# Chunks 1 and 2 of an attention and feed-forward kernel: their second matrix product by Strassen's seven products, with weights laid out by halves and other sums of weights on GpSimd

## The chip, the cores and the metric

The kernel runs on one core of a Trainium2 chip. A core has TensorE (matrix products into PSUM), VectorE, ScalarE and GpSimd (elementwise work), SyncE (SP, whose queue issues the DMAs here) and 16 DMA engines. The metric is the device time of one execution in microseconds (us). Less is better. The profile's names for the engines are PE (TensorE), PEld (its weight loads), DVE (VectorE), ACT (ScalarE), POOL (GpSimd) and SP.

## The reference

Eight sequences of 576 tokens go through windowed attention with eight heads of 64, and then through a feed-forward network with a hidden size of 2048.

```python
scores = scale * np.matmul(q, k.transpose(0, 1, 3, 2))
mask_plain = (rel >= 0) & (rel < window)                                # window 32, heads 0-3
mask_dil = (rel >= 0) & (rel < window * dilation) & (rel % dilation == 0)  # dilation 4, heads 4-7
...
attn = np.exp(scores - np.max(scores, axis=-1, keepdims=True))
attn = attn / (np.sum(attn, axis=-1, keepdims=True) + 1e-09)
out = np.matmul(attn, v)
...
h = x @ w_in                       # x: 4608 x 512, w_in: 512 x 2048
g = 0.5 * h * (1.0 + erf(h * inv_sqrt2))
return (g @ w_out).astype(np.float32)   # w_out: 2048 x 512
```

w_in and w_out come as 64-bit numbers, which the kernel decodes on the chip into a high and a low half in 32-bit form.

## The kernel before

**Tiling.** The 4608 tokens are nine chunks of 512: eight are the first 512 tokens of a sequence, the ninth holds the rests. A product keeps float32 accuracy by three passes (high by high, low by high, high by low), each of them 128x512 matmuls in fp32r. The weights are 16 tiles `weights[f]`, one for each 128 hidden columns. Each holds both layers, 512 numbers each, for both halves.

**Stages on TensorE.** Chunk 0 comes first, in an order written out by hand (`ORDER`): TensorE works on it while the weights are loaded, decoded by ScalarE (`k`, `j`) and VectorE (`w`), and while the attention of chunks 0 and 1 is worked out. A word such as `w13:v` is the next step of decoding tile 13 on VectorE; `h` and `o` are the first and second product for one tile on TensorE, `g` the GELU and its split into halves, `s l e i n t a x` the steps of attention (capitals for chunk 1). Then chunk 1 and chunk 2 are multiplied plainly from the weight tiles in SBUF (`chunk`, lines 995 and 1012), with 12 matmuls for each hidden tile and layer. The other six chunks go in three pairs (`two_chunks`): each layer is one Strassen step over the pair, that is seven products of half size (P1 to P7) instead of eight, for 8 hidden tiles of double width, with 6 matmuls each (lines 1135 and 1243), so 336 matmuls for a layer and a pair.

**What Strassen needs.** Four of the seven products take sums of weights. `prepare` makes them during chunks 1 and 2: two adds on GpSimd (line 722), four subtractions on VectorE (line 732), the high half on ScalarE (line 744), the low half on VectorE (line 747), and a DMA to a scratch in DRAM (`sums`). The plain parts go to DRAM too (`both`, `one`). Later the pairs fetch them as slabs (`ring`). On the token side, VectorE forms sums of x (line 1067) and of the hidden values (`sum_c`, line 1169), and each product's operand is split into halves by `split`: high on ScalarE (line 969), low on VectorE (line 976). Hidden values of a pair are kept as `c`, after their GELU on ScalarE (line 1119).

**What sets the order.** Behind `ORDER` a planner (`Flow`) places jobs on each engine by due times and costs; each engine runs its queue in that order, and waits where a semaphore says so. TensorE's own order is fixed by the program; at given times of its clock `pe` puts in visits of attention: the scores of two heads' pairs (line 332), and the products with the values (line 468 for chunk 2, 482 for later ones). The softmax between them (`attend`) is minimum (lines 366, 372), exponentials on ScalarE (line 380), inverse, scaling and transposes on VectorE (lines 389 to 422) and a move on ScalarE (line 841). For chunk 2 `xout` puts the result into the operand `x` (lines 500 and 503). Chunk 0's last copies out of PSUM are `store`.

Of the kernel before, what the change touches and what calls it, by code (L numbers as in the profile page):

```python
# [19 lines left out]
P = 128  # L20
# [18 lines left out]
ORDER = ("q0:d s0:p l0:v d0:d k0:a q1:d *36 s1:p w0:v l0:v w0:v w0:v d1:d k0:a q2:d q3:d w0:v e0:a e0:a j0:a k1:a v1:d "  # L39
# [17 lines left out]


class Flow:


    LAG, LAG_PE, TABLE, PULL, LATE, NEXT = 0.25, 0.5, 1.3, 0.06, 0.06, {"DVE": 0.1, "ACT": 0.03}
# [4 lines left out]
    def add(self, engine, time, do=None, after=(), due=0.0, begin=0.0, take=(), give=(), table="", land=0.0, issue=0.5):  # L67
        j = dict(engine=engine, time=time, do=do, after=list(after), due=due, begin=begin, take=list(take), give=list(give),
                 table=table, land=land, issue=issue, ready=0.0, then=[])
        self.jobs.append(j)  # L70
        return j
# [15 lines left out]
    def run(self):  # L87
# [7 lines left out]
        while there:  # L95
            best = None
            for j in there:
                at, e = self.start(j)
                if at is None:
                    continue  # L100
                turn = j["table"] not in ("", self.table)
                key = (round(at + self.PULL * max(0.0, j["due"] - at) - self.LATE * max(0.0, at - j["due"] - 2.0) + self.TABLE * turn, 2), j["due"])
                if best is None or key < best[0]:
                    best = (key, j, at + self.TABLE * turn, e)
# [30 lines left out]
        assert n == len(self.jobs), (list(self.held), [(j["engine"], j["due"], j["take"]) for j in there if j["engine"] != "DMA" or j["due"] < 480])  # L135
# [13 lines left out]
def attn_ffn(ctx: ExitStack, tc: tile.TileContext, qk, qk_lp, qk_ld, v, v_ld, w, outT):  # L149
# [85 lines left out]
    def weight_tile(f):  # L235
        if weights[f] is None:
            weights[f] = wpool.tile([P, 2, 2 * DM], F32R, tag="w", name="weight")
        return weights[f]

    def w_split(f):  # L240
        for cols in halves(f):
# [10 lines left out]
            nc.vector.scalar_tensor_tensor(weight_tile(f)[:, 1, cols], mid, 2.0 ** -36, t.bitcast(F32), op0=ALU.mult, op1=ALU.mult)  # L252

    def w_high(f):
        for cols in halves(f):
            e = yield
            copy(e, weight_tile(f)[:, 0, cols], raws[f][:, cols, 1].bitcast(F32))

# [162 lines left out]

    def turn_pe(s):
# [60 lines left out]
    def xout(s, px):  # L485
        yield {"ACT": 0.6}
        s.x = xg.tile([P, 2, N], F32R, tag="xg", name="x")
        if s.wide:
            put = []
            for b in range(2):  # L490
                src = px[:, :, b * 64:(b + 1) * 64].rearrange("p r (g i) -> p r g i", g=4)
                dst = [s.x[:, t].rearrange("p (r b i g) -> p r b g i", r=4, b=2, g=4)[:, :, b] for t in range(2)]
                put.append((src, dst))
        elif s.c < 2:
            put = [(s.px, [s.x[:, 0], s.x[:, 1]])]
# [911 lines left out]
```

## Time and profile before

| what | before |
|---|---|
| device time, 3 runs | 815.03, 816.36, 816.39 us, median 816.36 |
| profiled execution | 814.89 us, span 813.1 us |
| TensorE busy | 801.6 us, 99% of the span |
| VectorE, ScalarE, GpSimd busy | 598.7, 520.8, 57.3 us |
| DMA | 187 MB, mean 230 GB/s |

The profiled execution is one run; its span lies between its first and last instruction, and the remaining 1.8 us are around it. A busy share is an average over stages; the chain that ended last is the work that the end hung on, followed back from the last instruction. Matmuls are pipelined, so the time of one is read from a long run of them in the chain and not from the mean duration of a record.

### The profile page before, as it was taken

Reading aid. Unit: us, or ns where it says so; the run is one execution under the profiler, and the core shown is the slowest. Engines: PE = TensorE matmul, PEld = TensorE weight load, DVE = VectorE, ACT = ScalarE, POOL = GpSimd, SP = SyncE. Lnnn points to the kernel's source line nnn. Section 1 sums busy time; section 2 is a strip of 40 time slices with the busy share of each in tenths; the row PEclk is TensorE's granted clock in tenths of the full one; section 3 lists DMA queues with packets and bytes.
Section 4 is the critical chain, followed back from the end, with each engine's and each line's share of the span. In section 5 each row is a group of like instructions: output and inputs, shape, how many; then the busy total and the mean of one; then the engine's idle time right before and its main releaser. Section 6 shows DMA issues by size and latency. Waiting matters only on the chain.

```text
span 813.1 us, 19125 instructions
## 1 busy us (share of the span) xinstructions
PE 801.6 (99%) x7854; PEld 658.5 (81%) x7854; DVE 598.7 (74%) x1007; ACT 520.8 (64%) x1292; POOL 57.3 (7%) x78
## 2 busy tenths in 40 slices
PE   7999999999999999999999999999999999999998
PEld 5788888888888888888888887888888888888886
DVE  7999965877764846786798778866996853489673
ACT  8898853668865846888654479766754532565441
POOL 6000011513303100000000000000000000000000
PEclk9999999999999999999999999999999999999999
DMA  9972044877874788676784659759764399555102
GB/s 370 419 300 106 0 154 167 291 266 270 308 263 153 274 272 349 248 273 225 255 337 148 215 185 412 260 176 348 247 217 155 97 374 350 214 188 186 41 1 104
DMA packets 68647, 187.35 MB, mean 230 GB/s; under 512 B 4560, under 2 KB 33744, under 8 KB 56400
## 3 DMA queue, kind: packets, MB, share of 16 engines
q1 hardware_dynamic: 68560, 186.14, 63.0%
q8 instruction: 61, 1.00, 0.5%
q14 instruction: 26, 0.21, 0.1%
HBM read 144.44 MB, written 38.80 MB: 225 GB/s over the span
## 4 chain that ended last, share of the span: by engine, by line
PE 97%; ACT 2%; DMA 1%; DVE 0%; issue 0%; SPq 0%; DVEq 0%
PE ps L1135 28%; PE ps L1243 28%; PE ps L995 11%; PE ps L1012 11%; PE ps L514 6%; PE ps L534 5%; PE ps L332 3%; PE ps L482 2%; ACT sm L380 1%; PE ps L447 1%; DMA raw_w<-w 1%; PE ps L460 1%; PE ps L468 0%; ACT raw_w L233 0%; PE ps L429 0%; PE ps L318 0%
## 5 line engine op out<-in xcount | busy, mean ns | idle before, releaser
L1135 PE MATMUL ps<-parts,ring 128*128 128x512 f32 x1008 | 232.9, 391 | 0.0
L1243 PE MATMUL ps<-parts,ring 128*128 128x512 f32 x1008 | 230.4, 390 | 0.0
L1243 PEld LDWEIGHTS ps<-parts,ring 128*128 128x128 f32 x1008 | 188.8, 188 | 39.6 <-DVE parts L976 0.4
L1135 PEld LDWEIGHTS ps<-parts,ring 128*128 128x128 f32 x1008 | 188.2, 188 | 40.4 <-DVE c L1111 0.3
L969 ACT CAST parts<-c 128x512 fp32r<-128x512 f32 x168 | 100.9, 620 | 67.0 <-DVE parts L976 36.2
L976 DVE TENSOR_TENSOR parts<-c,parts 128x512 fp32r<-128x512 f32 x168 | 113.4, 688 | 31.5 <-ACT parts L969 30.1
L995 PE MATMUL ps<-x,weight 128*128 128x512 f32 x384 | 89.8, 391 | 0.0
L1012 PE MATMUL ps<-parts,weight 128*128 128x512 f32 x384 | 89.8, 391 | 0.0
L995 PEld LDWEIGHTS ps<-x,weight 128*128 128x128 f32 x384 | 71.5, 188 | 15.2
L1012 PEld LDWEIGHTS ps<-parts,weight 128*128 128x128 f32 x384 | 71.5, 188 | 15.2
L380 ACT ACTIVATE sm<-sm,st 128x64 f32<-128x64 f32 (+1 forms) x224 | 75.6, 340 | 7.6 <-DVE st L372 7.4
L1119 ACT ACTIVATE c<-c 128x512 f32<-128x512 f32 x96 | 57.7, 628 | 33.0 <-DVE c L1111 32.8
L1111 DVE TENSOR_TENSOR c<-c,ps 128x512 f32<-128x512 f32 x72 | 49.5, 688 | 27.6 <-PE ps L1135 25.1
L170 DVE COPY c<-ps 128x512 f32<-128x512 f32 x50 | 34.6, 692 | 46.7 <-PE ps L1135 46.3
L168 ACT COPY c<-ps 128x512 f32<-128x512 f32 x52 | 30.5, 587 | 57.4 <-PE ps L1135 50.0
L1169 DVE TENSOR_TENSOR c<-c 128x512 f32<-128x512 f32 x96 | 63.7, 684 | 0.0
L722 POOL TENSOR_TENSOR units<-weight 128x512 f32<-128x512 f32 x32 | 43.7, 1390 | 207.4 <-DVE g L526 99.6
L514 PE MATMUL ps<-x,weight 128*128 128x512 f32 x192 | 46.9, 394 | 0.0
L534 PE MATMUL ps<-g,weight 128*128 128x512 f32 x192 | 45.6, 390 | 0.0
L841 ACT COPY turned<-half 32x256 f32<-32x256 f32 x104 | 42.0, 404 | 5.5 <-DVE turned L422 4.0
L380 ACT ACTIVATION_READ_ACCUMULATOR sm<-sm,st 128x1 f32 x224 | 42.3, 189 | 0.0
L534 PEld LDWEIGHTS ps<-g,weight 128*128 128x128 f32 x192 | 36.0, 188 | 7.4
(99 smaller groups left out, 816.0 us busy)
## 6 DMA issues: line engine op xcount, KB each, us to landing
ring<-sums SPq DMA_DIRECT2D x48, 1024.0 KB, 6.5
ring<-both SPq DMA_DIRECT2D x24, 1024.0 KB, 6.9
v_sb<-v SPq DMA_DIRECT2D x17, 1024.0 KB, 9.2
raw_qk<-qk SPq DMA_DIRECT2D x32, 512.0 KB, 5.6
raw_w<-w SPq DMA_DIRECT2D x16, 1024.0 KB, 15.6
sums<-units SPq DMA_DIRECT2D x16, 1024.0 KB, 5.6
ring<-one SPq DMA_DIRECT2D x12, 1024.0 KB, 7.9
both<-weight SPq DMA_DIRECT2D x16, 512.0 KB, 6.6
```

The source lines that it names most:

```text
L380: nc.scalar.activation(t, s.sc[:, i // NU, at:at + 2 * KB] if s.c < 2 else t, AF.Exp, bias=s.st[:, 0, i:i + 1], scale=SCALE if s.c < 2 els ...
L514: nc.tensor.matmul(bank, weights[f][:, t, cc * P:(cc + 1) * P], x[:, xx], start=n == 0, stop=n == 3 * NC - 1)
L534: nc.tensor.matmul(ps[:, d], weights[f][:, t, DM + d * P:DM + (d + 1) * P], gs[f][:, u], start=first and n == 0, stop=last and n == 2)
L969: nc.scalar.copy(to if len(x.shape) == 2 else to.rearrange("p (g i) -> p g i", i=32), x)
L976: nc.vector.tensor_sub(a, x, b)
L995: nc.tensor.matmul(bank, weights[f][:, i, cc * P:(cc + 1) * P], x[:, j], start=n == 0, stop=n == 3 * NC - 1)
L1012: nc.tensor.matmul(ps[:, bank_of(acc[d])], weights[f][:, i, DM + d * P:DM + (d + 1) * P], made["g", c, f][:, j], start=f == 0 and n == 0, ...
L1111: nc.vector.tensor_add(C[f][:, part], C[f][:, part], ps[:, bank_of(bank)])
L1119: nc.scalar.activation(C[f][:, part], C[f][:, part], AF.Gelu)
L1135: nc.tensor.matmul(ps[:, bank_of(bank)], w()[:, a, i * P:(i + 1) * P], made[n, u, i][:, b], start=begins and k == 0, stop=k == 5, skip_gro ...
L1169: op(C[f][:, to], C[f][:, a], C[f][:, b])
L1243: nc.tensor.matmul(ps[:, bank_of((n, b, d))], w()[:, i, d * P:(d + 1) * P], made[key][:, j], start=begins and f == 0 and k == 0, stop=f == ...
```

## The change

Chunks 1 and 2 become a pair, pair 0, and there are four pairs. In pair 0 the first layer stays plain (a new branch for `n == 0` in `two_chunks`, line 1091 of the new file): 32 blocks of 12 matmuls, each with a GELU straight out of PSUM into `c` (line 1097). Its second layer takes the seven products as the other pairs do (line 1279). Chunk 2's attention comes earlier: scores and softmax of its first two pairs of heads stand at the end of `ORDER` (words with @), and the others in pair 0's first blocks.

A weight tile is now laid out by quarters with the high and low half side by side. Each tile is written to DRAM as it is decoded (`w_away`, words with z), 32 DMAs of 512 KB, which replace the 32 of `both` and `one`. Tiles 0 to 7 leave SBUF this way, and pair 0 fetches them back as `ring`. `prepare` now adds the high and low half of a tile on GpSimd (lines 778 and 784), and three VectorE subtractions follow in place of four (line 796). GpSimd's first add waits for the decoding of the last tile (`gate`). The high half may be made by VectorE too. The new names of the lines: 332, 380, 468, 841, 969, 976 and 1169 are now 370, 418, 516, 470, 1015, 1022 and 1198.

```diff
-    LAG, LAG_PE, TABLE, PULL, LATE, NEXT = 0.25, 0.5, 1.3, 0.06, 0.06, {"DVE": 0.1, "ACT": 0.03}
+    LAG, LAG_PE, TABLE, PULL, LATE, NEXT = 0.25, 0.5, 1.23, 0.02, 0.056, {"DVE": 0.1, "ACT": 0.03}
...
-            weights[f] = wpool.tile([P, 2, 2 * DM], F32R, tag="w", name="weight")
+            weights[f] = wpool.tile([P, 4, 2, DM // 2], F32R, tag="w", name="weight")
...
+    def w_away(t):
...
+        for layer in range(2):
+            to = drams["plain", layer, f // 4][2 * side:2 * side + 2, :, f % 4].rearrange("u p k -> p u k")
+            nc.sync.dma_start(to, weights[t][:, 2 * layer:2 * layer + 2].rearrange("p u t k -> p u (t k)").bitcast(F32))
...
-    NPAIRS = 3
+    NPAIRS = 4
...
+            turns = ((P1, every), (P4, every), (P2, range(4)), (P5, every), (P6, every), (P7, every), (P2, range(4, HALF)), (P3, every))
...
+        def join_side(side):
...
+            w = layer_0[f][side]() if layer == 0 else weights[tiles_of(f)[side]][:, 2:4]
+            nc.gpsimd.tensor_add(y(2 * side, 2 * side + 2), w[:, :, 0].bitcast(F32), w[:, :, 1].bitcast(F32))
...
+        if n == 0:
+            blocks = [(0, f) for f in range(5)] + [(1, f) for f in range(5)] + [(b, f) for f in range(5, HALF) for b in range(2)]
+            for b, f in blocks:
+                got = [fetch_layer_0(f)] if f > 3 else []
+                if b and f == 0:
+                    got += x_there["two", 0] + x_there["two", 2]
+                for side in range(2):
...
+                                nc.tensor.matmul(bank, column(w, i, cc), x[:, j], start=k == 0, stop=k == 3 * NC - 1)
...
+                        nc.scalar.activation(C[f][:, part], ps[:, bank_of(key)], AF.Gelu)
...
-    CH, PAIR = 384 * MM, 672 * MM
+    FIRST, PAIR = 720 * MM, 672 * MM
...
+    gate = const.tile([1, 8], F32)
+    nc.gpsimd.tensor_copy(gate, weights[NF - 1][0:1, 3, 1, 0:8].bitcast(F32))
+    for f in range(4):
+        prepare(1, f, 1.0 + 10.6 * f)
+        prepare(0, f, -1.2 + 8.0 * f)
+    for f in range(4, HALF):
+        prepare(1, f, 65.3 + 10.4 * (f - 4))
+        prepare(0, f, 76.6 + 11.4 * (f - 4))
-    chunk(1, ((0, 8), (8, 16)))
-    chunk(2, ((0, 8), (8, 16)))
```

TensorE's queue from the end of chunk 0 on, before (514, 534: chunk 0; 332: scores):

```order
L534 MATMUL ps<-g,weight 128x512 x36
L995 MATMUL ps<-x,weight 128x512 x12
L332 MATMUL ps<-raw_qk 32x64 x64
L995 MATMUL ps<-x,weight 128x512 x48
L332 MATMUL ps<-raw_qk 32x64 x64
L995 MATMUL ps<-x,weight 128x512 x36
L1012 MATMUL ps<-parts,weight 128x512 x12
```

The same place now (551 and 571 are chunk 0, 370 scores, 516 the products with the values):

```order
L571 MATMUL ps<-g,weight 128x512 x12
L370 MATMUL ps<-raw_qk 32x64 x64
L571 MATMUL ps<-g,weight 128x512 x24
L1091 MATMUL ps<-x,weight 128x512 x12
L370 MATMUL ps<-raw_qk 32x64 x64
L1091 MATMUL ps<-x,weight 128x512 x36
L516 MATMUL ps<-turned,v_sb 64x32 x64
L1091 MATMUL ps<-x,weight 128x512 x48
L1091 MATMUL ps<-x,ring 128x512 x12
L516 MATMUL ps<-turned,v_sb 64x32 x64
L1091 MATMUL ps<-x,ring 128x512 x12
L1091 MATMUL ps<-x,weight 128x512 x24
```

Chunk 2's first scores moved into chunk 0, and both of its products with the values now stand within the first nine blocks of pair 0.

ScalarE's queue between the second exponentials of chunk 2 and that second product, now (units are sums of weights, 1097 the GELU, 470 the move of the turned scores, 540 `xout`):

```order
L418 ACTIVATE sm_1798,st_1799<-sm_1798,st_1799 128x64 x3
L170 CAST units_1819<-units_1819 128x4x256
L1097 ACT_TABLE_LOAD
L1097 ACTIVATE c_1815<-ps_72 128x512
L1097 ACTIVATE c_1963<-ps_72 128x512
L170 CAST units_1917<-units_1917 128x4x256
L1097 ACTIVATE c_1963<-ps_72 128x512
L470 COPY turned_1986<-half_1970 32x256 x4
L1097 ACTIVATE c_2013<-ps_72 128x512
L470 COPY turned_2015<-half_1996 32x256 x4
L1097 ACTIVATE c_2013<-ps_72 128x512
L1097 ACTIVATE c_2095<-ps_72 128x512
```

Behind chunk 0 the same queue had before, with GELU and high half in turn:

```order
L1000 ACTIVATE gf_1619<-ps_72 128x512
L969 CAST parts_1624<-gf_1619 128x512
L1000 ACTIVATE gf_1644<-ps_72 128x512
L969 CAST parts_1647<-gf_1644 128x512
L1000 ACTIVATE gf_1667<-ps_72 128x512
L969 CAST parts_1671<-gf_1667 128x512
```

Two moves that TensorE's product waits for now stand behind casts for the sums of weights and GELUs.

VectorE's queue ahead of those two moves, now (796, 805: sums of weights; 443 to 460: scaling and transposes of the softmax):

```order
L443 TENSOR_TENSOR sm_1766<-sm_1766,st_1767 128x512
L805 TENSOR_TENSOR units_1819<-units_1819 128x4x256
L796 TENSOR_TENSOR units_1917<-units_1917 128x256
L427 TENSOR_SCALAR st_1799<-st_1799 128x8
L457 STREAM_TRANSPOSE half_1970<-sm_1766 128x256
L429 RECIPROCAL st_1799<-st_1799 128x8
L460 STREAM_TRANSPOSE turned_1986<-sm_1766 128x512
L443 TENSOR_TENSOR sm_1798<-sm_1798,st_1799 128x512
L805 TENSOR_TENSOR units_1917<-units_1917 128x4x256
L457 STREAM_TRANSPOSE half_1996<-sm_1798 128x256
L460 STREAM_TRANSPOSE turned_2015<-sm_1798 128x512
```

The low halves of two sums of weights stand between the steps of the softmax that the product waits for.

## Rows read from the trace of the kernel before

**Rows 1.** The page: busy time by engine, and TensorE's granted clock.
```profile
PE 801.6 (99%) x7854; PEld 658.5 (81%) x7854; DVE 598.7 (74%) x1007; ACT 520.8 (64%) x1292; POOL 57.3 (7%) x78
...
PEclk9999999999999999999999999999999999999999
```

**Rows 2.** Chain that ended last: start us, us, what.
```profile
118.11 8.16 PE ps L534 x36
126.27 2.72 PE ps L995 x12
128.99 1.41 PE ps L332 x91
...
188.30 2.00 PE ps L468 x128
...
411.34 46.24 PE ps L1243 x204
...
733.24 76.17 PE ps L1243 x336
```

**Rows 3.** Waits of TensorE, 126 to 814 us: total, times, longest.
```profile
PE ps L482 <- issue: 0.2, 1, 0.2
PE ps L332 <- issue: 0.2, 1, 0.2
```

**Rows 4.** Busy time by stretch, count in brackets; then clock, DMA share, GB/s.
```profile
24.00:126.30 102.30, 102.30 (x891) 84.79 (x886) 90.21 (x136) 82.62 (x157) 2.77 (x2) 1.00 0.46 182
126.30:324.90 198.60, 198.44 (x2561) 162.90 (x2560) 135.61 (x237) 134.21 (x384) 40.96 (x30) 1.00 0.76 266
...
411.30:491.10 79.80, 79.80 (x594) 65.61 (x593) 65.74 (x111) 44.72 (x102) 0.00 (x0) 1.00 0.61 218
```

**Rows 5.** ScalarE and VectorE by form: shape, count, busy us, mean ns, idle before.
```profile
L976 DVE TENSOR_TENSOR parts<-c,parts 128x512 fp32r<-128x512 f32 x168 | 113.4, 688 | 31.5 <-ACT parts L969 30.1
...
L1000 ACT ACTIVATE gf<-ps 128x512 f32<-128x512 f32 x32 | 19.1, 597 | 29.6 <-PE ps L995 28.1 <-DVE parts L976 1.5
...
L744 ACT CAST units<-units 128x1024 fp32r<-128x1024 f32 x16 | 16.7, 1044 | 1.7 <-issue 1.6
...
L380 ACT ACT_TABLE_LOAD x8 | 10.3, 1283 | 0.1
```

**Rows 6.** ScalarE in time: start us, us, instruction, idle before it.
```profile
154.86 0.35 ACT L380 ACTIVATE sm<-sm,st 128x64 f32<-128x64 f32 x1
155.11 0.19 ACT L380 ACTIVATION_READ_ACCUMULATOR sm<-sm,st 128x1 f32 x1
155.21 0.33 ACT L380 ACTIVATE sm<-sm,st 128x64 f32<-128x64 f32 x1
```

**Rows 7.** ScalarE in time, behind the product with the values.
```profile
190.36 1.08 ACT L500 CAST x<-ps 128x512 fp32r<-128x512 f32 x2 [0.78 <-PE ps L468]
191.47 1.65 ACT L841 COPY turned<-half 32x256 f32<-32x256 f32 x4
```

**Rows 8.** GpSimd's adds in time.
```profile
143.05 3.00 POOL L722 TENSOR_TENSOR units<-weight 128x512 f32<-128x512 f32 x2 [9.96 <-ACT parts L969]
...
184.81 3.52 POOL L722 TENSOR_TENSOR units<-weight 128x512 f32<-128x512 f32 x2 [5.22 <-DMA sums<-units]
```

**Rows 9.** VectorE in time, beside those adds.
```profile
143.56 1.34 DVE L976 TENSOR_TENSOR parts<-gf,parts 128x512 fp32r<-128x512 f32 x1
...
146.73 1.22 DVE L747 TENSOR_TENSOR units<-units 128x1024 fp32r<-128x1024 f32 x1
```

**Rows 10.** VectorE in time, beside the later adds.
```profile
185.15 2.04 DVE L747 TENSOR_TENSOR units<-units 128x1024 fp32r<-128x1024 f32 x1
187.11 1.78 DVE L976 TENSOR_TENSOR parts<-gf,parts 128x512 fp32r<-128x512 f32 x1
```

**Rows 11.** The page: DMA issues, KB each, median us to landing.
```profile
sums<-units SPq DMA_DIRECT2D x16, 1024.0 KB, 5.6
...
both<-weight SPq DMA_DIRECT2D x16, 512.0 KB, 6.6
```

More of the change, by code (lines that the diff above doesn't have):

```diff
@@ L134, in run @@
                     there.append(k)
-        assert n == len(self.jobs), (list(self.held), [(j["engine"], j["due"], j["take"]) for j in there if j["engine"] != "DMA" or j["due"] < 480])
+        assert n == len(self.jobs)
 def at_once(gen):
@@ L422, in turn, with moved, move @@
         nc.vector.transpose(s.t, x[:, :, 0].unsqueeze(1).broadcast_to((P, 2, 2 * NU, KB)))
+    def moved(s):
+        yield
+        move(s)
+    def move(s):
+        for r in range(4):
+            to = r ^ 1
+            nc.scalar.copy(s.t[32 * to:32 * to + 32, r % 2], s.half[32 * r:32 * r + 32])
     def turn_pe(s):
@@ L556, in job @@
         kind, i = name[0], name[1:]
+        if kind == "@":
+            p = int(i[1:])
+            if i[0] == "v":
+                return load_v(xs[2][p])
+            if i[0] == "S":
+                return together([scores(xs[2][p + k], 6) for k in range(2)])
+            return dict(l=lowest, e=softmax, i=inverse, n=norm, t=turn, m=moved)[i[0]](xs[2][p])
         if kind == "d":
@@ new lines, in attn_ffn, with fetch_layer_0, go @@
+    SUMS = ((P5, P4, P7, P6), (P5, P7, P4, P6))
+    IN_SUMS = SUMS[0]
+    PLAIN = ({P1: 0, P2: 1, P3: 3}, {P1: 0, P2: 2, P3: 3})
+    def slab_of(layer, u, i):
+        if u in IN_SUMS:
+            return drams["sums", layer, i][SUMS[layer].index(u)]
+        return drams["plain", layer, i][PLAIN[layer][u]]
+    put_in, joined, layer_0, fetched_0 = {}, {}, {}, {}
+    for f in range(4):
+        layer_0[f] = [lambda t=t: weights[t][:, 0:2] for t in tiles_of(f)]
+    def fetch_layer_0(f):
+        if f not in fetched_0:
+            st = {}
+            def go():
+                st["w"] = wpool.tile([P, 4, 2, NW1], F32R, tag="w", name="ring")
+                nc.sync.dma_start(st["w"].rearrange("p u t k -> p u (t k)").bitcast(F32),
+                                  drams["plain", 0, 1][:, :, f % 4].rearrange("u p k -> p u k"))
+            layer_0[f] = [lambda side=side: st["w"][:, 2 * side:2 * side + 2] for side in range(2)]
+            at = 22 + 6 * (f - 4) if f < 5 else 44 + 11 * (f - 4)
+            key = ("layer 0", f)
+            fetched_0[f] = flow.add("DMA", 2.6, go, [joined[k, f - 4] for k in range(2)], due=at - 8, begin=at - 20, take=[("w", key), ("ring", ("r",) + key)], land=2.3)
+        return fetched_0[f]
@@ L725, in plain @@
-        def plain():
-            one, two = (g, f) if layer == 0 else (f, g)
-            part = slice(cols.start + NW1, cols.stop) if layer == 0 else slice(cols.start, cols.start + NW1)
-            nc.sync.dma_start(drams["both", layer, half][:, f % 4 * 2:f % 4 * 2 + 2], weights[two][:, :, cols].bitcast(F32))
-            nc.sync.dma_start(drams["one", layer, half][:, f % 4 * 2:f % 4 * 2 + 2], weights[one][:, :, part].bitcast(F32))
-        def both(op, to, a, b):
-            return lambda: op(y(to), y(a), y(b))
@@ L733, in prepare @@
-        sums = []
-        for i in range(2):
-            sums.append(flow.add("POOL", 1.35, add_up(i), sums[:], due - 6, due - 12,
-                                 [] if i else [("prep", key + ("prep",)), ("w", key)]))
-        away = [flow.add("DMA", 2.0, plain, due=due, begin=due - 12, land=2.3, issue=1.2)]
-        sub, add = nc.vector.tensor_sub, nc.vector.tensor_add
-        j = sums
-        for op, to, a, b in ((sub, B22, B22, B12), (sub, B12, B12, B11), (add, B11, B22, B11), (sub, B21, B21, B11)):
-            j = [flow.add("DVE", 0.37, both(op, to, a, b), j, due - 3)]
@@ L894, in attend @@
             up = ("upper", c, p, 0)
-            visit = flow.add("PE", 1.45, pe_work([scores(s, 6), scores(t, 6)]), q, take=[("upper", up)], give=[x for _, x in keys])
-            visits.append((scores_at[0], visit))
+            visit = q is not None and flow.add("PE", 1.45, pe_work([scores(s, 6), scores(t, 6)]), q, take=[("upper", up)], give=[x for _, x in keys])
+            if visit:
+                visits.append((scores_at[0], visit))
             lows = []
-            for i, o in enumerate(pairs):
+            for i, o in enumerate(pairs if visit else ()):
                 low, tt = softmax_of(i, o, [visit], scores_at[0] + i * 1.4, exps_at[i])
@@ L1401 @@
     out = r.results[0]["outT"].T
-    one, two = out[:3 * N].reshape(3, N, DM), out[3 * N:].reshape(3, 2, 2, 8, 32, DM)
-    two = two.transpose(0, 2, 3, 1, 4, 5).reshape(6, N, DM)
-    chunks = np.concatenate([one, two], 0)
+    chunks = out.reshape(NCH, N, DM)
     parts = chunks[:B], chunks[B].reshape(B, REST, DM)
```

357 lines of the change are left out of this document (177 added, 180 removed), and 36 rows, old and new, of the table ORDER.

## The prediction

> **What bounds the kernel now.** I read the page first. TensorE is busy for 99% of the span and its granted clock is at the top in each slice [rows 1]. Busy records overlap, so that share proves little, and I went on to the chain that ended last. From 118 us to the end it is made of TensorE's runs alone, one behind the other: chunk 0's last products, the plain products of chunks 1 and 2, the visits of attention, and the Strassen layers [rows 2]. The waits of TensorE say the same from the other side: between 126 and 814 us it waited for no other engine, and its two entries of 0.2 us are its own issue [rows 3]. So each matmul that goes away is worth its whole time, as long as nothing else becomes late. A run of 336 matmuls takes 76.17 us in the last layer [rows 2], which is 0.2267 us for one.
>
> The second thing to read is how much room the engines have that feed TensorE. In the stretch of chunks 1 and 2 VectorE is busy for 135.6 of 198.6 us, with 237 instructions (0.572 us each), and in the second Strassen layer of the pair behind it for 65.7 of 79.8 us, with 111 instructions (0.592 us each) [rows 4]. There TensorE waited for nothing at 82%.
>
> **The change part by part.**
>
> *What is removed.* Before, chunks 1 and 2 took 768 large matmuls, 384 for each layer. Now the first layer keeps 384 and the second takes 7 products of 8 tiles with 6 matmuls, 336. In all, TensorE's queue holds 3120 large matmuls in place of 3168; the small ones of attention are the same in number. 48 x 0.2267 = 10.9 us off the path. That follows from the order and is not in doubt. Against the profiled execution (814.9 us) this gives 804.0, and against the median of the three runs (816.4, which is 1.5 us above the profiled one) 805.5. I go by the median.
>
> *What is moved into chunk 0.* The scores of chunk 2's first pairs cost 1.41 us wherever they stand [rows 2]. Their exponentials now come ahead of pair 0. Chunk 0's h15 ends at 118.1 us [rows 2]; o13, the scores, o14 and o15 follow, 3 x 2.72 + 1.41, and a few tenths behind the scores, so pair 0 begins at F = 127.8 us. On ScalarE 16 exponentials take 0.33 us each, since each one's reading of the sum overlaps the next [rows 6], so 5.3 us, behind a table load of 1.28 us [rows 5] that can run early. With two moves of 1.65 us [rows 7], the VectorE steps between them and two copies out of PSUM, I get ScalarE free at about F + 6.0. The GELUs that wait behind this free PSUM banks. Six banks hold six blocks of 2.72 us, 16 us, so TensorE doesn't notice. I cost this at nothing; without those banks it would be 6.0 - 2.7 = 3.3 us.
>
> *Chunk 2's second product with the values.* This is where a wait is likeliest. It stands behind 108 large matmuls, one scores visit of 1.41 us and one product of 2.00 us, so at F + 28.3 with the few tenths behind each visit. On ScalarE there stand, between F + 6.0 and the move that it needs: four casts for sums of weights (1.04 us each), three table loads (1.28 each), seven GELUs (0.60 each) [rows 5], 16 exponentials (5.3), two casts of x (1.08) and two moves (3.3) [rows 6, 7]. Together 4.2 + 3.8 + 4.2 + 5.3 + 1.1 + 3.3 = 21.9, so F + 27.9. The margin is 0.4 us. VectorE has 34 instructions between the scores (F + 4.3) and the last transpose; at 0.572 us each 19.4 us of the 22 us to F + 26.3, where the last move has to start. Both queues are nearly full, and they hand work to each other.
>
> Here GpSimd matters. Beside its adds VectorE is slower: a subtraction that takes 0.69 us [rows 5] took 1.34 within two adds [rows 8, 9], 0.33 us for an add, and beside two later adds a low half took 2.04 in place of 1.22 and a subtraction 1.78 in place of 0.69 [rows 5, 8 to 10], 0.95 us for an add. By the order GpSimd has 12 adds that can run before F, and four whose buffers only come free from the first puts (5.6 us to land [rows 11]), which puts them into this stretch. Four adds at 0.33 to 0.95 us cost 1.3 to 3.8 us, less the margin 0.9 to 3.4; if they fall into gaps, nothing. I take 0.6 us for an add, between the rows, so 2.4 - 0.4 = **2.0 us**. The operand x of chunk 2 comes out of this product: ScalarE and VectorE need some 2.5 us, and one block of 2.72 us stands in front of the block that reads it. I cost it at nothing; it is late by what exceeds 0.2 us.
>
> *The rest of pair 0's first layer.* It lasts 87.1 us of matmuls and ten visits (5 x 1.41 + 2 x 2.00 + 3 x 1.41), 102.3 us. VectorE's 129 instructions make 73.8 us by 0.572. The later products with the values have 2 us of room and more by the same way of counting, and a wait of 2 us earlier adds to that. Nothing.
>
> *The second layer of pair 0.* 76.2 us of matmuls and three visits give 80.4 us. VectorE's queue from the first split of the hidden values to the last has 129 instructions, at 0.592 us each 76.4 us, or 95%. Some of that can run before the layer begins, since chunk 1's hidden values are ready early. I take nothing, with 0 to 3 us for the range.
>
> *The DMAs.* The 32 writes of plain weights, 512 KB each [rows 11], go from the stretch of chunks 1 and 2 into chunk 0, where the DMA engines were busy for 46% [rows 4]. In SP's queue two loads of weights and the loads of chunk 2 now stand behind some of them. The tiles written first had been decoded long before, so SP doesn't wait for them; if it did, the decoding of tiles 12 and 14 would wait with it. The 22 more slab loads of 1 MB go into a stretch at 76%, less what moved out. Nothing.
>
> Sum: 816.4 - 10.9 + 2.0 = **807.5 us**.
>
> **The rivals.**
>
> *A: no new wait.* The adds fall into gaps of VectorE: 805.5 us. For it speaks that the planner's queues left TensorE without a wait in every stage of before [rows 3]; against it that no stage of before had ScalarE without a gap for 22 us ahead of a product.
>
> *B: VectorE becomes the bound in the second layer.* If its instructions take 0.65 us there (0.688 us is the mean of a split alone [rows 5], neighbours overlap), 129 make 83.9 us for 80.4 us; with the same late start as in the forecast that is 4 to 7 us, so 812 us. Against it: at 82% there was no wait at all.
>
> *C: the sums of weights come late.* The second layer's products P4 need slabs of sums, 10.9 us into the layer. A slab has GpSimd, VectorE, ScalarE, a put of 5.6 us and a fetch behind it, and all stand in queues with the softmax. If the last tiles were late by some 10 us the gain would be gone: 816 us, no change. By the order the last put stands two visits ahead of the layer, which speaks against it.
>
> *D: GpSimd holds VectorE for the whole of each add, and more adds fall here.* The first 12 adds wait for buffers that chunk 0's last products free. If they too slip behind F, and each add of 1.5 us [rows 8] holds VectorE for its whole length, 12 adds cost 18.0 - 0.4 = 17.6 us: 823 us, slower. It is slower than before by over 0.2% (818.0) from 9 adds on (9 x 1.5 - 0.4 = 13.1 us lost against 10.9 gained). Against it speak the rows: 0.65 us lost beside two adds, 1.9 beside two others, not 3.0.
> [...]
>
> **How the numbers follow.** Forecast 0.55, A 0.18, B 0.13, C 0.07, D 0.07. The range takes the forecast's bounds (805.5 + 0 to 3.4, and 0 to 3 in the second layer), A and most of B: 804.8 to 813.5, where the lower end is A less 0.7 us, half the spread of the three runs. A measurement of this kernel can tell about 0.2% (1.6 us) from no change. Faster by more: the forecast, A and B, 0.86; within it: C, 0.07; slower: D, 0.07.
>
> **What would show it.** Right: in the chain of waits TensorE waits once for ScalarE's move, about 28 us into pair 0, for 1 to 3 us, and else for nothing over 1 us; the run of pair 0's second layer has 336 matmuls in 76 us apart from its visits; VectorE is over 90% busy there. Wrong: TensorE waiting for VectorE's splits all through the second layer (B), for a slab behind a put (C), or VectorE's two-input instructions beside GpSimd at twice to three times their length in the first 28 us (D). If the clock fell in some stretch for a wait, the matmuls would take longer than 0.2267 us there, and the sum would be wrong in its first term.

## The result, and the profile after

| kernel | device time, median (us) | runs | ratio to before, 95% interval |
|---|---|---|---|
| before | 815.8 (814.8 to 817.1) | 11 | |
| changed | 820.7 (816.2 to 823.4) | 11 | 1.0056 (1.0043 to 1.0070) |

The change made the kernel slower by 0.56%; the forecast was 1.1% faster. Its runs spread over 7.2 us, those of before over 2.3, and the mean granted clock of its runs lies between 0.987 and 0.996. What follows is the account of one of them, the profiled one (0.992). Its execution took 819.8 us, with a span of 817.9 us against 813.1. The page now shows 48 large matmuls fewer, as worked out, TensorE no longer covering the span, and VectorE at 652.8 us in place of 598.7 [rows 1].

```profile
span 817.9 us, 19149 instructions
...
PE 799.4 (98%) x7806; PEld 655.3 (80%) x7806; DVE 652.8 (80%) x1072; ACT 531.7 (65%) x1305; POOL 60.5 (7%) x75
...
q8 instruction: 61, 1.00, 0.5%
```

The waits of TensorE between 126 and 814 us, which were 0.4 us before [rows 3], come to 7.6 us (columns: instruction, what it waited for, total us, times, longest):

```profile
PE ps L508 <- issue: 4.0, 2, 2.2
PE ps L1279 <- ACT sm L418: 2.2, 1, 2.2
PE ps L530 <- ACT parts L1015: 0.7, 1, 0.7
PE ps L516 <- ACT turned L470: 0.5, 1, 0.5
PE ps L370 <- issue: 0.2, 1, 0.2
```

The stage lengths say where the time went. From the first matmul of a stage to the first of the next, in us, with the pairs numbered as in the changed kernel:

| stage | before | changed | what was expected |
|---|---|---|---|
| pair 0 (chunks 1 and 2), both layers | 198.6 | 195.1 | 188.2 |
| pair 1, both layers | 166.2 | 165.5 | 166.2 |
| pair 2, first layer | 85.3 | 85.3 | 85.3 |
| pair 2, second layer | 80.7 | 88.2 | 80.7 |
| pair 3, both layers | 152.1 | 152.1 | 152.1 |

The expected 188.2 is 198.6 less 10.9, less 1.5 for the scores that moved into chunk 0 (1.41 and a tenth behind them), plus the 2.0 of the forecast wait. Two places lost what was missing: 6.9 us in pair 0, and 7.5 us in a stage that the change doesn't touch; pair 1 gave 0.7 back.

**The untouched stage.** In pair 2's second layer stand the two visits of chunk 8's products with the values, 192 small matmuls each (line 508, before 460). Here is TensorE in time around them, first in the kernel before (start us, us, instruction, number of matmuls):

```profile
580.40 2.11 PE L460 MATMUL ps<-turned,v_wide 32*64 32x32 f32 x192
582.44 9.81 PE L1243 MATMUL ps<-parts,ring 128*128 128x512 f32 x42
592.19 2.04 PE L460 MATMUL ps<-turned,v_wide 32*64 32x32 f32 x186
```

and then in the changed kernel, where in brackets stands the idle time ahead of a row:

```profile
577.51 1.77 PE L508 MATMUL ps<-turned,v_wide 32*64 32x32 f32 x156
581.04 0.57 PE L508 MATMUL ps<-turned,v_wide 32*64 32x32 f32 x36 [1.76 <-issue]
581.54 14.19 PE L1279 MATMUL ps<-parts,ring 128*128 128x512 f32 x54
595.66 1.83 PE L508 MATMUL ps<-turned,v_wide 32*64 32x32 f32 x165
599.69 0.66 PE L508 MATMUL ps<-turned,v_wide 32*64 32x32 f32 x27 [2.20 <-issue]
```

Both visits stop in the middle, behind 156 and 165 matmuls, and wait for nothing that the profile can name ("issue"). From 578.3 us until TensorE went on at 581.04 the DMA engines moved nothing but one packet of the queue that the page calls "instruction", and that one had landed at 579.56. This is the DMA view of 578.3 to 579.4 us:

```profile
DMA packets 1, 0.02 MB, mean 15 GB/s; under 512 B 0, under 2 KB 0, under 8 KB 0
...
q8 instruction: 1, 0.02, 5.5%
```

And behind each stop the granted clock fell from 1.00 to 0.50 for 3.41 us (582.69 to 586.10 and 599.76 to 603.17). In the changed kernel by stretch (us; busy time of TensorE, its weight loads, VectorE, ScalarE and GpSimd with counts; granted clock; DMA share; GB/s):

```profile
578.90:580.70 1.80, 0.38 (x37) 0.26 (x24) 1.80 (x4) 0.00 (x0) 0.00 (x0) 1.00 0.00 0
...
582.50:585.90 3.40, 3.40 (x11) 2.57 (x10) 1.38 (x2) 1.20 (x4) 0.00 (x0) 0.53 0.91 316
```

The second row is the stretch at half clock. It lies in a run of 54 large matmuls, which took 14.19 us; the same 54 take 12.55 in a run below (e1) whose clock didn't fall. So the stage lost 4.0 us standing and some 3.4 us at half the clock (half of 3.4 us, twice).

**Pair 0.** The forecast wait is there: the second product of chunk 2 with the values (line 516) stops half way for ScalarE's late move, and lasts 159.79 - 155.89 = 3.9 us in place of 2.0 [rows 2].

```profile
155.89 1.87 PE L516 MATMUL ps<-turned,v_sb 64*64 64x32 f32 x68
158.30 1.56 PE L516 MATMUL ps<-turned,v_sb 64*64 64x32 f32 x60 [0.54 <-ACT turned L470]
159.79 4.44 PE L1091 MATMUL ps<-x,ring 128*128 128x512 f32 x12
```

The third row was not forecast: the 12 matmuls behind it took 4.44 us, most of it at a granted clock of 0.50 (159.44 to 162.85 us), where the same row takes 3.02 us in e1 and e5 below. And at the seam of pair 0's two layers TensorE waited again:

```profile
235.13 1.75 PE L530 MATMUL ps<-v_sb,turned 64*32 64x64 f32 x128 [0.70 <-ACT parts L1015]
236.81 1.66 PE L1279 MATMUL ps<-parts,ring 128*128 128x512 f32 x6
240.71 5.51 PE L1279 MATMUL ps<-parts,ring 128*128 128x512 f32 x16 [2.24 <-ACT sm L418]
```

The 2.24 us are put down to ScalarE's exponentials, but six matmuls of the layer had already run, so no first operand was missing; the experiments name another cause. Behind it the clock fell to 0.50 for 3.41 us too (241.36 to 244.77), and 16 matmuls took 5.51 us in place of 3.8. Last, VectorE is nearly full in pair 0's first layer:

```profile
127.00:237.00 110.00, 108.34 (x1668) 88.37 (x1667) 102.71 (x159) 85.69 (x243) 32.96 (x19) 0.98 0.93 341
237.00:322.00 85.00, 82.76 (x718) 67.16 (x718) 72.27 (x123) 51.86 (x134) 0.00 (x0) 0.98 0.76 281
```

102.7 of 110 us, with the DMA engines at 0.93. In the kernel before the same 110 us had 80.7 and 0.78. The second row is pair 0's second layer.

### The profile page after: what moved, and what is told of

It is laid out like the page before. It is cut to its first block, busy times and chain, and to the rows that moved or that the text cites. A ratio compares the mean times of both kernels' runs of the same rounds, so it can differ in the third digit from the quotient of the medians.

```text
span 817.9 us, 19149 instructions
## 1 busy us (share of the span) xinstructions
PE 799.4 (98%) x7806; PEld 655.3 (80%) x7806; DVE 652.8 (80%) x1072; ACT 531.7 (65%) x1305; POOL 60.5 (7%) x75
## 4 chain that ended last, share of the span: by engine, by line
PE 82%; DVE 7%; ACT 3%; DMA 3%; issue 2%; SPq 1%; POOL 1%; DVEq 0%; POOLq 0%; ACTq 0%
PE ps L1279 38%; PE ps L1164 28%; PE ps L551 5%; PE ps L571 5%; PE ps L370 2%; ACT sm L418 2%; DVE units L796 2%; DMA units<-plain 2%; PE ps L530 1%; DVE units L805 1%; PE ps L495 1%; DMA raw_w<-w 1%; DVE sm L404 1%; DMA sums<-units 1%; DVE sm L443 1%
## 5 line engine op out<-in xcount | busy, mean ns | idle before, releaser
L1279 PE MATMUL ps<-parts,ring 128*128 128x512 f32 x1344 | 312.8, 394 | 2.2 <-ACT sm L418 2.2
L1279 PEld LDWEIGHTS ps<-parts,ring 128*128 128x128 f32 x1344 | 254.7, 190 | 57.1 <-ACT sm L418 2.7
L1164 PE MATMUL ps<-parts,ring 128*128 128x512 f32 x1008 | 232.9, 391 | 0.0
L1164 PEld LDWEIGHTS ps<-parts,ring 128*128 128x128 f32 x1008 | 188.2, 188 | 40.3 <-DVE c L1141 0.3
L1015 ACT CAST parts<-c 128x512 fp32r<-128x512 f32 x224 | 135.5, 621 | 100.5 <-DVE parts L1022 47.9
L1022 DVE TENSOR_TENSOR parts<-c,parts 128x512 fp32r<-128x512 f32 x224 | 151.4, 687 | 51.7 <-ACT parts L1015 49.7
L1198 DVE TENSOR_TENSOR c<-c 128x512 f32<-128x512 f32 x128 | 89.2, 711 | 0.1
L172 DVE COPY c<-ps 128x512 f32<-128x512 f32 x56 | 38.7, 691 | 42.6 <-PE ps L1164 42.2
L170 ACT COPY c<-ps 128x512 f32<-128x512 f32 x48 | 28.2, 588 | 47.1 <-PE ps L1164 39.8
L551 PE MATMUL ps<-x,weight 128*128 128x512 f32 x192 | 46.9, 394 | 0.0
L1091 PE MATMUL ps<-x,ring 128*128 128x512 f32 x192 | 46.8, 401 | 0.0
L1091 PE MATMUL ps<-x,weight 128*128 128x512 f32 x192 | 45.0, 392 | 0.0
L1091 PEld LDWEIGHTS ps<-x,ring 128*128 128x128 f32 x192 | 36.7, 193 | 8.1
```

The source lines that it names most:

```text
L551: nc.tensor.matmul(bank, column(weights[f], t, cc), x[:, xx], start=n == 0, stop=n == 3 * NC - 1)
L1015: nc.scalar.copy(to if len(x.shape) == 2 else to.rearrange("p (g i) -> p g i", i=32), x)
L1022: nc.vector.tensor_sub(a, x, b)
L1091: nc.tensor.matmul(bank, column(w, i, cc), x[:, j], start=k == 0, stop=k == 3 * NC - 1)
L1164: nc.tensor.matmul(ps[:, bank_of(bank)], w()[:, a, i * P:(i + 1) * P], made[n, u, i][:, b], start=begins and k == 0, stop=k == 5, skip_gro ...
L1198: op(C[f][:, to], C[f][:, a], C[f][:, b])
```

## The theories

**I, instruction packets.** TensorE's instructions are fetched in packets by DMA: 61 packets, 1.00 MB, on the page, for 7806 matmuls and as many weight loads, so about 256 instructions in a packet of 16 KB. A burst of small matmuls uses one up in 1.45 us (156 matmuls ran in 1.77 us, above, and a packet holds 128 with their weight loads). Where two packet boundaries stand in one burst, the second packet isn't there in time. The stops would then depend on where the boundaries fall, and the change moved those by taking 96 instructions out ahead of them.

**II, the visits themselves.** Their loads, the planner's new weights or a buffer make the visits wait.

**A, GpSimd beside VectorE** makes VectorE slower in pair 0, and so the products with the values late. **B**, its rival: the sums' own instructions, queued ahead of the softmax, make them late.

One thing can be read off without an experiment. I numbered all records of TensorE's queue in the trace (weight loads, matmuls, semaphore instructions) in order of time. The three stops that begin at 238.5, 579.3 and 597.5 us end at the records 6081, 13249 and 13761. The distances are 28 x 256 and 2 x 256 exactly, and each number leaves 193 when divided by 256; below, a boundary is a record with such a number. So the wait at 238.5 us, which the profile gave to ScalarE, belongs to the same kind: a packet landed at 239.5, and TensorE went on at 240.7.

## The experiments

**The same kernel with its packet boundaries moved (e1).** 60 more tiny matmuls at the start of TensorE's stream:

```diff
-BURN = 5
+BURN = 65
```

> The changed kernel with 60 more tiny matmuls (32x64, on constants, 120 instructions with their weight loads) at the very start of TensorE's stream, where it idles for its first loads anyway; all else the same. Theory I (TensorE's instructions come in packets of 256, and the two stops of 1.98 and 2.42 us in the middle of the value visits of chunk 8 stand where the second packet boundary inside one burst of small matmuls is met before its packet is there): the boundaries move 120 instructions earlier, none of the two bursts holds two of them any more, both stops go (-4.0 us) and with them the two 3.4 us stretches at half clock behind them (-3.4 us): 820.7 - 7.4 = 813.3 us; if the 2.6 us stop at 238 goes as well with its half clock, 809.5 us. Theory II (the stops belong to those visits: their loads, the order around them or a buffer): 820.7 us, with stops at the same matmuls.

812.2 us (6 runs), ratio 0.9966 (0.9952 to 0.9980). In the profiled run both visits run through, the clock is 1.000 over the span (0.993 to 0.998 in the other five), and the stop at 238 is gone too:

```profile
576.24 2.12 PE L508 MATMUL ps<-turned,v_wide 32*64 32x32 f32 x192
578.29 12.55 PE L1279 MATMUL ps<-parts,ring 128*128 128x512 f32 x54
590.77 1.96 PE L508 MATMUL ps<-turned,v_wide 32*64 32x32 f32 x176
```

Theory II falls: neither loads nor order nor planner were touched. The 809.5 us expected for the case that the stop at 238 goes too were missed by 2.7; pair 0 stayed long for other reasons, as the last experiments show. With its boundaries here the change is 0.3% faster than the kernel before.

**The kernel before, with the boundaries moved into its visits (e2)**, BURN = 85:

> The kernel before with 80 more tiny matmuls (160 instructions) at the start of TensorE's stream. Theory I: in the kernel before the boundaries happen to stand near the start of the wide visits; moved 160 instructions earlier, a pair of boundaries falls into each of the two wide value visits as in the changed kernel, so two stops of about 2 us and two stretches of 3.4 us at half clock: 815.8 + 7.4 = 823 us (at least +4 if the clock doesn't fall). Theory II: 815.8 us, no stop.

824.5 us (4 runs), ratio 1.0115 (1.0092 to 1.0138). The kernel before gets the stops:

```profile
581.67 1.80 PE L460 MATMUL ps<-turned,v_wide 32*64 32x32 f32 x160
585.09 0.46 PE L460 MATMUL ps<-turned,v_wide 32*64 32x32 f32 x32 [1.61 <-issue]
585.48 11.40 PE L1243 MATMUL ps<-parts,ring 128*128 128x512 f32 x42
596.81 2.01 PE L460 MATMUL ps<-turned,v_wide 32*64 32x32 f32 x180
601.81 0.33 PE L460 MATMUL ps<-turned,v_wide 32*64 32x32 f32 x12 [2.98 <-issue]
```

Its stage took 88.9 us for 80.7, with two stretches of 3.4 us at half clock. Most of the rest was lost ahead of chunk 1, which TensorE began 1.05 us later.

**The price of the extra matmuls (e3)**, the kernel before with BURN = 29:

> The kernel before with 24 more tiny matmuls (48 instructions) at the start: tells what the extra matmuls themselves cost. Theory I: with this shift no burst holds two boundaries at a bad place, so 815.8 us (within 0.5). Theory II: 815.8 us as well; anything else would say that the matmuls at the start have a price of their own.

815.7 us, ratio 1.0009 (1.0000 to 1.0019): at most 0.2%, and no wait over 0.3 us. What the other shifts did is not the matmuls' own cost.

**A small dose (e7)**, the changed kernel with BURN = 21:

> The changed kernel with 16 more tiny matmuls (32 instructions) at the start, a small dose of the shift. Theory I (packets of 256 instructions): the stops move 16 matmuls earlier in the two wide value visits, to behind 140 and 149 of their 192; the first packet boundary in the first visit comes to stand 12 matmuls behind its start instead of 28, so its packet is asked for before the visit and the first stop shrinks to under 1 us; the second stop (boundary 21 matmuls behind the start) stays at 1.5 to 2.5 us. Theory II (the stops belong to the visit): both stops stay at 2.0 and 2.4 us behind 156 and 165 matmuls.

One run, 822.2 us. The stops moved exactly as far as the stream did, to behind 140 and 149 matmuls, and both shrank:

```profile
581.31 1.64 PE L508 MATMUL ps<-turned,v_wide 32*64 32x32 f32 x140
583.91 0.75 PE L508 MATMUL ps<-turned,v_wide 32*64 32x32 f32 x52 [0.96 <-issue]
...
598.67 1.70 PE L508 MATMUL ps<-turned,v_wide 32*64 32x32 f32 x149
601.90 0.80 PE L508 MATMUL ps<-turned,v_wide 32*64 32x32 f32 x43 [1.52 <-issue]
```

It was no faster: in pair 0 a visit met a boundary 10 matmuls ahead of its end and stood for 4.2 us, and 1.2 us were lost at another boundary at 199 us.

**Two more shifts (e9, e10)**, 96 and 140 instructions, with BURN = 53 and 75:

> The changed kernel with 48 more tiny matmuls (96 instructions) at the start, a second shift at which no value visit of chunk 8 holds two packet boundaries with the first well inside it. Theory I (packets of 256 instructions): no stops in the wide visits and a clock of 1.000 there, 812 us within 1.5, as with the shift by 120. Theory II (the gain of the shift by 120 was something else that the 60 matmuls did): another time, up to 820.7 us.

> The changed kernel with 70 more tiny matmuls (140 instructions) at the start. The shift by 96 freed the wide value visits but showed stops in pair 0 where a packet boundary follows another too closely (at 188.4, 198.5 and 234.7, 4.8 us and 3.4 us of half clock), the shift by 120 none there. Theory I: at 140 fewer boundaries stand close to one another in pair 0's visits than at 96, and none in the wide ones, so 811 to 813 us, with whatever stops are left at packet boundaries alone; if the time between a packet's request and its landing in pair 0 is longer than the 3.5 to 5 us seen, up to 815 us.

814.5 us (10 runs), 0.9983 (0.9968 to 0.9997), and 813.6 us (10 runs), 0.9981 (0.9961 to 1.0002). Both have the wide visits free of stops, so the gain of e1 was no accident of its 60 matmuls; but e9 missed its 812 us by more than the 1.5 allowed. What is left differs in pair 0. At 96 these waits stand there:

```profile
PE ps L530 <- issue: 2.5, 1, 2.5
PE ps L370 <- issue: 2.3, 1, 2.3
```

and with a third of 0.4 us at 189 us they are at the record numbers 4545, 4801 and 5825. At 140 the longest wait is one that the profile puts down to VectorE's splits:

```profile
PE ps L1279 <- DVE parts L1022: 2.4, 3, 2.0
```

The longest of the three ends at 318.7 us at record 7617, a boundary, 1.3 us behind the landing of a packet. Over all these kernels, shifted by 0 to 160 instructions, each wait of 0.3 us or more behind 126 us that the profile puts down to "issue" is at a boundary. (In the next run, e4, one of 11.1 us is not.)

**GpSimd's adds as DMAs (e4).** A first attempt at theory A let DMA copies take the place of the adds of line 784. (AV(2,2) in what was expected here and below is the visit of line 516 that waits; AV(3,0) and AV(4,0) are the visits of line 530 at 195 and 235 us.)

```diff
-            nc.gpsimd.tensor_add(y(2 * side, 2 * side + 2), w[:, :, 0].bitcast(F32), w[:, :, 1].bitcast(F32))
+            nc.sync.dma_start(st["q"][:, 2 * side:2 * side + 2].bitcast(F32), w.bitcast(F32))
```

> The changed kernel with the 24 joining adds that GpSimd makes straight from weight tiles replaced by copies of the tile by DMA of the same shape, so that the sums are without the added half (the output is not the reference's); the order on TensorE, VectorE and ScalarE is the same, and TensorE's stream has the same instructions. Theory A (the value visit AV(2,2) came 2.0 us late because VectorE ran slower beside GpSimd's adds): the visit starts on time, 2.0 us and the 1.7 us of half clock behind it go, and some of the 0.7 us wait at 235: 820.7 - 4 = 817 us. Theory B (it came late because the sums' work on VectorE and ScalarE stands ahead of the softmax in their queues): the visit stays at least 1 us late, 820 us or so; the copies take longer to land than an add takes, so the sums may also be later than before.

864.3 us. TensorE waited up to 11.1 us in pair 0's visits, for loads of values (7.2 us) and scores (2.0 us) among others, so the run says nothing on A or B. It adds transfers where the DMA engines were at 0.93 already.

**Without the 24 adds of line 784 (e5)**, with the stream shifted as in e1; VectorE reads the halves of the tile itself, and the four adds of line 778 stay:

```diff
-            nc.gpsimd.tensor_add(y(2 * side, 2 * side + 2), w[:, :, 0].bitcast(F32), w[:, :, 1].bitcast(F32))
+            st[side] = w
...
-            return lambda: nc.vector.tensor_sub(y(*to), y(*a), y(*b))
+            return lambda: nc.vector.tensor_sub(y(*to), *((y(*a), y(*b)) if layer and f > 3 else [st[1][:, :, k].bitcast(F32) for k in range(2)] if len(to) > 1 else (st[a[0] // 2][:, a[0] % 2:a[0] % 2 + 1, 0].bitcast(F32), y(*b))))
```

> The changed kernel with 60 more tiny matmuls at the start (as the run that shifted its instruction packets, 812.2 us) and without the 24 GpSimd adds that join a tile's high and low halves: VectorE's differences read the tile's halves as they are instead (the joined sums are missing, so the output is not the reference's). Order, shapes and counts on TensorE, VectorE and ScalarE are the same. Theory A (VectorE is slowed by GpSimd's adds beside it, 16 us in the first layer of pair 0, and so the value visits AV(2,2), AV(3,0), AV(4,0) and some plain products wait): the waits of 1.6, 1.2 and 1.2 us and the 2.5 us of small ones go or nearly: 812.2 - 5 = 807 us. Theory B (the sums' own instructions, queued ahead, delay the visits; the slowing costs nothing): no more than 1 us off, 811 to 812 us.

807.0 us (4 runs), ratio 0.9901 (0.9886 to 0.9916): 5.2 us less than e1, as theory A had it. All waits for the products with the values are gone, though the sums' instructions stand ahead of the softmax as before; so B alone does not make the visit late. What is left of TensorE's waits is a slab:

```profile
PE ps L1279 <- DMA ring<-sums: 1.2, 1, 1.2
PE ps L1279 <- issue: 0.2, 1, 0.2
```

(The record that waits for the slab happens to be at a boundary, but that packet had landed 14 us before.)

**The adds put back, for nobody (e8).** Either the adds disturb VectorE, or VectorE no longer waits for them. So the 24 adds run again, but write where nothing reads:

```diff
-            st[side] = w
+            st[side] = w; nc.gpsimd.tensor_add(st["q"][:, 2 * side:2 * side + 2, 0].bitcast(F32), w[:, :, 0].bitcast(F32), w[:, :, 1].bitcast(F32))
```

> The kernel without joining adds (807.0 us) with GpSimd's 24 adds put back, of the same size and from the same tiles, but written into the half of the scratch tile that is overwritten later, so that VectorE's differences don't wait for them (the output is still without the joined sums). Theory A1 (VectorE and GpSimd working at the same time is what costs: VectorE's operations get longer beside an add): the time comes back to about 812 us, with VectorE's differences 0.5 to 1 us longer where an add runs beside them. Theory A2 (what the run without adds gained is that the differences no longer waited for GpSimd): 807 us, within 1.

811.1 us (4 runs), ratio 0.9946 (0.9927 to 0.9964): 4.0 us of the 5.2 are back. The visit of line 516 is late again, 162.02 - 157.62 = 4.4 us, with the half clock behind it:

```profile
157.62 1.86 PE L516 MATMUL ps<-turned,v_sb 64*64 64x32 f32 x68
160.01 2.08 PE L516 MATMUL ps<-turned,v_sb 64*64 64x32 f32 x60 [0.54 <-ACT turned L470]
162.02 4.21 PE L1091 MATMUL ps<-x,ring 128*128 128x512 f32 x9
```

In pair 0's first layer VectorE waits for GpSimd nowhere in this run, and five of its differences of 128x256 took 1.39 to 1.51 us beside an add, for 0.42 without. So for the visit of line 516 it is the two engines working at once, A1. The later visits run through here, while two were late in e1; that pair 0 is as long as in e1 all the same (192.8 for 192.9 us, 188.7 in e5) is for the most part the clock's doing, which fell for 6.8 us here and not there. So for the later visits the waiting, A2, may have a part; the intervals of the total don't settle it.

**The softmax ahead of the sums (e6)**, in the shifted kernel:

```diff
+            for x in (low + exp + inv + norms + j + turns) if (c, p) == (2, 2) else []:
+                x['late'] = 1.0
```

> The shifted changed kernel (812.2 us) with one planner weight changed: the steps of the softmax of chunk 2's second duo, which AV(2,2) waits for, gain priority once they are late (1.0 instead of 0.056), so VectorE does them ahead of the sums' differences that stood before them; what is computed stays the same. Theory B (the visit is late because of what stands ahead of it on VectorE, and that wait is a loss of its own): AV(2,2) starts on time and 1.6 us go: 810.6 us. Theory C (VectorE is full through the whole first layer of pair 0, so a wait that is taken away here comes back at a later visit or at a split): AV(2,2) on time, but AV(3,0), AV(4,0) or the start of the second layer later by as much: 812.2 us, within 0.7.

816.5 us (10 runs), ratio 1.0008 (0.9992 to 1.0023), 4.2 us slower than e1 and slower than either theory had it. The edit did more than was meant: the planner now puts the visit of line 516 two blocks, 24 large matmuls, earlier into TensorE's queue. There it no longer waits for a move, but for a packet; and work is missing later:

```profile
PE ps L1281 <- ACT parts L1017: 3.1, 2, 2.6
PE ps L530 <- ACT turned L470: 2.2, 2, 1.7
PE ps L516 <- issue: 1.1, 1, 1.1
```

(1281 and 1017 are 1279 and 1015.) The 2.6 us at 248 us are a split that came late; the other 0.5 us of that row are at a boundary, 7617. That is the way of the expectation's theory C, at a larger price; since TensorE's order and the boundaries moved too, the run shows the direction and not the size.

## Why the prediction was wrong

**The 48 matmuls: right, and too little to look at.** They are gone, and the stages around them got shorter. The step that failed is the sentence that a matmul that goes away is worth its whole time as long as nothing else becomes late, together with the small matmuls being left out because they were "the same in number". Their number stayed, their place in the instruction stream did not. The first wide visit began at record 13025 in the kernel before, with one boundary inside; now at 12936 (89 and not 96 earlier, since semaphore instructions were added), with boundaries behind some 28 and 156 of its 192 matmuls. In the kernel before the second visit also held two boundaries, behind 4 and 132 matmuls, without a stop: the first one stood so near the start that the transfer of the second one's packet began at 590.6 us, during the slow large matmuls ahead of the visit (592.2). The visit's place decides, and no row that I read shows that place. The numbers of the records do: the stops at 6081, 13249 and 13761 lie at multiples of 256 from each other. The page of before counts the packets too (q8 instruction: 61, 1.00 MB), so a stop between two of them should have stood beside the others as a rival: two stops of 2 us and what the clock adds, on either kernel.

**The accounting.** 13.7 us lie between the span that the steps give (813.1 - 10.9 + 2.0 = 804.2) and the measured 817.9:

| cause | us | shown by |
|---|---|---|
| packet stops in the two wide visits | 4.0 | e1, e2, e7 |
| half clock behind them | 3.4 | e1, e2 |
| packet stop at 238.5 and half clock behind it | 2.2 + 1.7 | record number, e1 |
| half clock behind the visit of line 516 | 1.4 | the trace; e5 |
| line 530's visit at 235 later by | 1.0 | the trace |
| a packet stop at 205 | 0.4 | record number |
| the visit of line 516, against the forecast | -0.1 | the trace |
| pair 1, against the kernel before | -0.7 | stage lengths |
| the rest | 0.4 | not shown |

Nearly 12 of the 13.7 us come from instruction packets.

**Chunk 2's second product with the values: right in place and mechanism, and near in size.** Forecast 2.0 us, measured 1.9, in the only wait for line 470. Ten adds had run before pair 0 began, and four fell into the stretch, as forecast. Beside them these rows of VectorE are longer (start, us):

```profile
142.74 2.21 DVE L805 TENSOR_TENSOR units<-units 128x1024 fp32r<-128x1024 f32 x1
...
148.37 1.49 DVE L796 TENSOR_TENSOR units<-units 128x256 f32<-128x256 f32 x1
149.78 1.78 DVE L443 TENSOR_TENSOR sm<-sm,st 128x512 f32<-128x512 f32 x1
151.48 1.21 DVE L805 TENSOR_TENSOR units<-units 128x1024 fp32r<-128x1024 f32 x1
```

with these adds of GpSimd beside the first three, and none beside the last:

```profile
142.24 3.85 POOL L784 TENSOR_TENSOR units<-weight 128x512 f32<-128x512 f32 x2 [14.90 <-PE ps L516]
148.28 2.72 POOL L784 TENSOR_TENSOR units<-weight 128x512 f32<-128x512 f32 x2 [2.19 <-DMA sums<-units]
```

2.21 for 1.21 us, 1.49 for 0.42, 1.78 for 0.69 (the last two by the median of such rows without an add): 3.1 us for four adds, 0.8 us for one, where I took 0.6. Less the margin of 0.4 that would be 2.7 us, so that 1.9 came so near 2.0 is in part luck. In the single records each of the three rows ends behind the end of the add that was running when it began, by 1.08, 0.28 and 0.55 us, a little less than it takes alone; and the second add, 2.28 us long where most take 1.3, ends behind the first of these rows in the same way. So in these rows the one that came second stood until the other was done. That is how rival D had an add hold VectorE, and in the second add it goes the other way round; the price for an add stayed below the add's own length because one of the four waited for VectorE instead, and the others had run for 0.1 to 0.5 us when VectorE's row began. Other rows of the changed kernel took beside an add what they take without one: reductions (line 410) 0.67 to 0.69 us for a median of 0.68, transposes 0.43 and 0.45 for 0.44 (line 457) and 0.67 for 0.67 (line 460), a cast (line 172) 0.69 for 0.69, and rows that read PSUM (line 404) 0.67 to 0.69 for 0.68.

**What was left out behind that wait.** I costed a wait by its own length. Here the clock fell behind it, and the 12 matmuls that followed took 1.4 us more. The last sentence of the forecast's part on what would show it named that, without a price.

**The rest of pair 0's first layer: wrong.** "73.8 us of 102.3" for VectorE was a count of instructions by an average. The trace has 102.7 of 110 us. Some of it is the sums of hidden values that start early; some 16 us are the lengthening beside the 18 adds of that stretch (rows of lines 427, 443, 796, 805 and 1198, against the median of their kind without an add). The busy share alone does not tell who is late: without the adds (e5) it is still 99.3 of 110 us, since later work moves up. In the second layer VectorE was then busy for 72.3 of 85 us, 85% where the forecast had 95%. In e1, where packets don't interfere, two later products with the values were late by 1.2 us each, and pair 0 still took 192.9 us for the 188.2 expected; without the adds (e5) it took 188.7. So the wait that I forecast as one has followers, and the step "nothing" was worth 4.7 us there.

**The DMAs: "nothing" is doubtful.** On the page the packets stand among the DMA queues, at 0.5% of the 16 engines' span. From the point where TensorE is 43 instructions from a boundary to the start of the next packet's transfer it took 4.8 us on average for the 13 packets of pair 0's first layer (127 to 237 us), at a DMA share of 0.93, and 3.9 us in e1, at 0.92. In the same 110 us of the kernel before it took 2.0 us, at 0.78; but with its boundaries shifted it took 1.8 us (e2) and 3.7 us (e3), at 0.77. So the place of the boundaries moves this time too, and no run changed the load by itself. That the load lengthens it is argued and not shown.

**The rivals.** A's place without a wait was not reached; B's waits for splits are 0.4 us in e1; C's late slab is there in small, 1.2 us in e5, 1.0 in e10 and 0.4 in e8; D's condition was not met, since ten adds had run before pair 0 began. The result was slower by a cause that none of them had.

## What to carry to other kernels

A burst of small matmuls can be bounded by the fetch of its own instructions; here two bursts of 192 stood for 1.8 and 2.2 us. Number the records of TensorE's queue in a trace, find the remainder by 256 from one stop (193 here), mark each such record, and see whether two marks fall into one burst; any edit ahead of it moves the marks, so compare two kernels at more than one such phase before judging an edit worth 1% (here the changed kernel took 820.7, 814.5, 813.6 or 812.2 us by the phase). A wait of TensorE can cost nearly its own length again through the clock (here 6.2 us of packet stops and 5.1 us of half clock behind them), and elementwise work given to GpSimd is paid for in part by VectorE's own SBUF operations beside it (here 24 adds that nobody read cost 4.0 us).

## What the runs showed of the hardware

In each of eight kernels' traces (53 or 54 packets each behind 100 us; 53 in the changed kernel and in the one before), no packet's transfer began while TensorE was more than 43 instructions short of the boundary ahead of that packet's own (43 in the kernel before, 41 in the changed one). So in these traces TensorE had, when a transfer began, at most those 43 instructions and one packet of 256 ahead of it. A transfer took 0.9 to 1.9 us (0.9 to 1.6 in the changed kernel), and in each stop of over 1 us the first instruction of the packet ran 1.2 to 1.5 us after its end (1.2, 1.5 and 1.4 in the changed kernel's three). The first wide visit of the changed kernel has the whole chain: TensorE came within 43 instructions of its first boundary at 577.55 us, the second one's packet moved from 578.60 to 579.56, and TensorE, which had run dry at 579.28, went on at 581.04.

What makes the clock fall is not settled. Behind the visit of line 516 it fell where the visit lasted 3.9 us (changed kernel), 4.4 (e8) and 3.6 (e10), and not where it lasted 3.6 (e1, e7) or 3.8 (e9), so the length of the wait alone does not decide it.
